# A planned order of attention pairs with groups of two, and filler matmuls in TensorE's planned gaps, in a two-layer decode kernel

## Chip, cores, metric

One core of a Trainium2 chip (trn2). The metric is device time in microseconds of one execution. Every time quoted is from runs of state "fast" unless it is said otherwise; a median of all runs is given where it helps.

## The reference, cut to what matters

```python
# x = A_x                        four tokens (B=4, one position each), D=448
x = x + A_ref(layernorm(x), K, V, wq, wo)   # attention: 16 query heads on 8 KV heads, Dh=256,
x = x + B_ref(layernorm(x), wg, wu, wd)     #   window = last 2048 cache rows
x = x + A_ref(layernorm(x), K, V, wq, wo)   # the same caches and weights again: layer 1
x = x + B_ref(layernorm(x), wg, wu, wd)     # feed-forward, F=1792, silu(x wg) * (x wu) @ wd
```

There are 4 tokens x 8 KV heads x 2 layers = 64 "pairs" of attention. A pair reads 1 MB of K and 1 MB of V. Layer 1 reads what layer 0 read, so a cache half (512 KB) that stays in SBUF saves a load.

## The kernel before

The kernel is a graph of operations with planned durations. A list scheduler written in Python orders them for each engine, gives loads one of 27 half-tiles, and places semaphore waits; the chip then runs five fixed instruction streams. The parts that matter (cuts marked `# ...`):

```python
NPOOL = 27                       # half-tiles of 512 KB
KEEP_K = 5; KEEP_V = 5           # heads per token whose K / V stay for layer 1
KLEAD = 2.2; KTAIL = 0.4; VLAG = 1.3; SLEAD = 2.5; FR = 8.4; FRD = 8.4; WOR = 0.4
ROWF = (0, 1, 2)                 # tokens whose feed-forward runs in row form

def schedule(self, npool):
    # ... at each step: the engine that is free first takes the ready operation of lowest rank
            o = min((o for o in avail[e] if ready_at[o] <= t + 1e-9), key=lambda o: (o.rank, o.i))
            if o.cell is not None:                 # a cache load: the half-tile that comes free first
                slot = min(pool)
                pool.remove(slot)
                # ... the load waits for the operation that releases this half-tile
            avail[e].remove(o)
            o.start = t
            free[e] = t + o.dur
    # ...

def pair(pos, si, side, nside, t, layer, kvh):     # one token, layer, head
    # two K loads, each followed by a VectorE transpose:
    g.op(DVE, 1.18, pos, tr, w=(kk[hf],))
    # two V loads; then on PE 32 score matmuls (8 columns of weights, 128 moving columns)
    o = g.op(PE, 0.87, pos - SLEAD, scores, r=tuple(kk) + (f"qe{q_}",), w=(f"s{s_}",), bank=(f"S{s_}",))
    if not keep_k: o.rel = tuple(kc)               # scores release K
    # max (VectorE), spread (PE), negated max (VectorE), exp (ScalarE), turn (PE), copy (ScalarE),
    # sum (PE, VectorE), then 2 x 8 value matmuls, which release V, and the combine
    # (ScalarE copy, VectorE subtract, PE flip, VectorE scale)

def steps():   # tokens two by two: layer 1 of token t-1 beside layer 0 of token t, shifted by three heads
    ...
```

Of the kernel before, what the change touches and what calls it, by code (L numbers as in the profile page):

```python
# [26 lines left out]
KEEP_K = 5  # L27
KEEP_V = 5
SHIFT = 3


KLEAD = 2.2
KTAIL = 0.4
VLAG = 1.3
SLEAD = 2.5
FR = 8.4
FRD = 8.4
WOR = 0.4
# [3 lines left out]
NY = 3  # L42
TRP = 1
LAND = 1.5
DSTART = 2.1
ROWF = (0, 1, 2)
MMV = 0.034
FAR = 1e30
TAIL = {"pe": 0.2, "dve": 0.12, "act": 0.15, "pool": 0.1, "sp": 0.05}
# [8 lines left out]

class Op:
    __slots__ = ("i", "eng", "dur", "rank", "emit", "deps", "succ", "nbytes", "dsem", "dval",  # L60
                 "start", "end", "pos", "waits", "inc", "val", "known", "run", "cell", "rel")

    def __init__(self, i, eng, dur, rank, emit):
        self.i, self.eng, self.dur, self.rank, self.emit = i, eng, dur, rank, emit
        self.deps = {}
        self.succ = []
        self.nbytes = 0
        self.dsem = None
        self.dval = 0
        self.cell = None  # L70
        self.rel = ()
        self.inc = False
        self.val = 0
        self.waits = []


class Graph:
    def __init__(self):
        self.ops = []
        self.writer = {}  # L80
        self.readers = {}
        self.banks = {}
        self.dcount = {}
# [6 lines left out]
    def op(self, eng, dur, rank, emit, r=(), w=(), bank=(), acc=()):  # L90

        o = Op(len(self.ops), eng, dur, rank, emit)
        self.ops.append(o)
# [39 lines left out]
    def schedule(self, npool):  # L133
        same = 0.08
        for o in self.ops:
            for d in o.deps:
                d.succ.append(o)
# [9 lines left out]
        order = {e: [] for e in avail}  # L147
        n = 0
        while n < len(self.ops):
# [16 lines left out]
            if o.cell is not None:  # L166
# [5 lines left out]
                if slot[2] is not None:  # L172
                    o.deps[slot[2]] = True
            avail[e].remove(o)
            o.start = t
            free[e] = t + o.dur
            o.end = t + o.dur
            if o.nbytes:
                chan = max(chan, t + DSTART) + o.nbytes / 16 * (0.007 / o.run + 1 / 26.6e3)
                o.end = chan + LAND - TAIL[SP]  # L180
# [15 lines left out]
        self.span = max(o.end for o in self.ops)  # L196
        self._place_waits()

# [46 lines left out]
def orders():  # L245



    keep = max(KEEP_K, KEEP_V)
    tail = list(range(SHIFT))  # L250
    first, second = [], []
    order = list(range(HKV))
    for t in range(B):
        first.append(order)
        mid = order[HKV - keep:] + [h for h in order[:HKV - keep] if h not in tail]
        mid = [h for h in mid if h not in tail]
        second.append(mid + tail)
        order = tail + mid
    return first, second


def steps():



    first, second = orders()
    out = [((0, 0, h),) for h in first[0]]
    for t in range(1, B):
        for i, h in enumerate(first[t]):
            if i >= SHIFT:  # L270
                assert second[t - 1][i - SHIFT] == h
                out.append(((t - 1, 1, h), (t, 0, h)))
            elif t > 1:
                assert second[t - 2][HKV - SHIFT + i] == h
                out.append(((t - 2, 1, h), (t, 0, h)))
            else:
                out.append(((t, 0, h),))
    out += [((B - 2, 1, h),) for h in second[B - 2][HKV - SHIFT:]]
    return out + [((B - 1, 1, h),) for h in second[B - 1]]


def build(nc, A_x, A_k_cache, A_v_cache, A_wq, A_wo, B_x, B_w_gate, B_w_up, B_w_down, out):
# [3 lines left out]
    with ExitStack() as es:  # L286
# [10 lines left out]
        tiny = sb("tiny", [128, 12 + NS], BF16)  # L297
        onesb, qmask, osel, rsel = tiny[:, 0:1], tiny[:, 2:6], tiny[:, 6:8], tiny[:, 8:12]
        pmax = [tiny[:, 12 + s:13 + s] for s in range(NS)]
        far = sb("far", [128, 16, 2], BF16)  # L300
        tsel = sb("tsel", [128, 4, B], BF16)
        selt = [sb(f"selt{h}", [128, 2, 4, 2, 2], BF16) for h in range(2)]
        small = sb("small", [128, 11 + 2 * NS + 4 * NY + B + 4], FP32)
        rmask = small[:, 11 + 2 * NS + 4 * NY:11 + 2 * NS + 4 * NY + B]
        rvec = small[:, 11 + 2 * NS + 4 * NY + B:11 + 2 * NS + 4 * NY + B + 4]
        nmask = small[:, 9 + 2 * NS + 4 * NY:11 + 2 * NS + 4 * NY]
        onesf, wrow, lomask = small[:, 0:1], small[:, 1:5], small[:, 5:6]
        expo = small[:, 6 + 2 * NS + 4 * NY:9 + 2 * NS + 4 * NY]
        negm = [small[:, 6 + 2 * i:8 + 2 * i] for i in range(NS)]
        rs = [small[:, 6 + 2 * (NS + i):8 + 2 * (NS + i)] for i in range(NY)]  # L310
        ri = [small[:, 6 + 2 * (NS + NY + i):8 + 2 * (NS + NY + i)] for i in range(NY)]
        qc = [sb(f"qc{t}", [128, HKV, 8, 2], BF16) for t in range(B)]
        qe = [sb(f"qe{i}", [128, 8, 4, 2], BF16) for i in range(NQ)]
        qS = sb("qS", [128, 128], BF16)
# [7 lines left out]
        xe = sb("xe", [128, 2, B], BF16)  # L322
# [5 lines left out]
        praw = [sb(f"praw{s}", [128, 258], BF16) for s in range(NS)]  # L328
        pT = [sb(f"pT{s}", [128, 2, 2, 4, 2, 2], BF16) for s in range(NY)]
        oh = [sb(f"oh{s}", [128, DH], BF16) for s in range(2)]  # L330
# [26 lines left out]
        def c_fill(e):  # L357
            e.memset(onesf[:, :], 1.0)
            e.memset(expo[:, 0:1], -0.5)
            e.memset(expo[:, 1:3], -1.0)  # L360
# [5 lines left out]
            e.memset(xn[:, :, :], 0.0)  # L366
            return e.memset(Ab[:, :], 0.0)
# [7 lines left out]
        for a in range(4):  # L375
            g.op(DVE, 0.1, R0, lambda e, a=a: e.memset(qmask[32 * a:32 * a + 32, a:a + 1], DH ** -0.5), r=("qmask",),
                 w=(f"qmask{a}",))
        ivt = identb[:, :].rearrange("p (h x z n) -> p h x z n", h=2, x=2, n=2)
        for h in range(2):
            for y in range(2):  # L380
                for x in range(2):
                    g.op(DVE, 0.1, R0, lambda e, h=h, y=y, x=x: e.tensor_copy(selt[h][:, x, :, y, :], ivt[:, h, x, 0:4, :]),
                         r=("identb",), w=(f"selt{h}{y}{x}",))
        idq = identb[:, :].rearrange("p (q z n) -> p q z n", q=4, n=2)
        g.op(DVE, 0.2, R0, lambda e: e.tensor_reduce(
            nmask[:, :], idq[:, :, 0:4, :].rearrange("p q a n -> p n q a"), AX.XY, ALU.add), r=("identb",), w=("nmask",))
        g.op(DVE, 0.1, R0, lambda e: e.tensor_reduce(negm[0][:, 0:1], nmask[:, :], AX.X, ALU.add), r=("nmask",), w=("negm0",))
        g.op(DVE, 0.1, R0, lambda e: e.tensor_scalar(negm[0][:, 1:2], negm[0][:, 0:1], -2.0, 1.0, op0=ALU.mult, op1=ALU.add),
             r=("negm0",), w=("negm0",))
        g.op(DVE, 0.1, R0, lambda e: e.tensor_scalar(  # L390
            far[:, :, :], nmask[:, :].unsqueeze(1).broadcast_to([128, 16, 2]), negm[0][:, 1:2], FAR, op0=ALU.add, op1=ALU.mult),
            r=("nmask", "negm0"), w=("far",))
        for s_ in range(NS):
            g.op(DVE, 0.2, R0, lambda e, s_=s_: e.memset(Sb[s_][:, :], 0.0), w=(f"s{s_}",), bank=(f"S{s_}",))
            g.op(DVE, 0.2, R0, lambda e, s_=s_: e.memset(praw[s_][:, :], 0.0), w=(f"praw{s_}",))
# [6 lines left out]
        iv = identb[:, :].rearrange("p (j y n) -> p j y n", j=4, n=2)  # L402
        g.op(DVE, 0.2, R0, lambda e: e.tensor_reduce(
            osel[:, :], iv[:, :, 0:2, :].rearrange("p j y n -> p n j y"), AX.XY, ALU.max, negate=True), r=("identb",),
            w=("osel",))
        g.op(DVE, 0.2, R0, lambda e: e.tensor_reduce(lomask[:, :], iv[:, :, 1, :], AX.XY, ALU.add), r=("identb",),
# [33 lines left out]
        def norm(t, rank, x):  # L440
# [15 lines left out]
            vec(rank, lambda e: e.tensor_copy(s[:, 12:14], Z2[:, 0:2]), ("z2",), (k + "m",), 0.09, ("Z2",))  # L456
# [30 lines left out]
        def qproj(ts, rank):  # L487
# [39 lines left out]
            vec(rank, lambda e: e.tensor_copy(qS[:, 0:32 * n], Zb[:, 0:32 * n]), ("z",), ("qS",), 0.12, ("Z",))  # L527
# [10 lines left out]
            g.op(PE, 0.45, rank, select, r=("qS", "identb"), w=("z2",), bank=("Z2",))  # L538
# [176 lines left out]
        first, second = orders()  # L715
        seq = [p for s in steps() for p in s]
# [6 lines left out]
        def pair(pos, si, side, nside, t, layer, kvh):  # L723
            p_, s_, q_ = pos % NY, pos % NS, pos % NQ
            if layer == 1 and (t, kvh) in k_held:
                kc, kk = k_held.pop((t, kvh))
            else:
                kc, kk = [[], []], [f"k{pos}_{hf}" for hf in range(2)]
                ksrc = A_k_cache[t, kvh, s0:s0 + WIN, :].rearrange("(p j) d -> p (j d)", p=128)
                for hf, cell in enumerate(kc):  # L730
                    g.dma(pos - KLEAD if pos <= LAST1 else pos + KTAIL, 1 << 19, lambda e, cell=cell, hf=hf: e.dma_start(  # L731
                        half[cell[0]][:, :], ksrc[:, 2048 * hf:2048 * hf + 2048]), None, w=(kk[hf],), run=4096, cell=cell)

                    def tr(e, cell=cell):
                        a = half[cell[0]][:, :].bitcast(UINT32).rearrange("p (k s) -> p k s", k=32)
                        return e.transpose(a, a)  # L736
                    g.op(DVE, 1.18, pos, tr, w=(kk[hf],))
            if layer == 1 and (t, kvh) in v_held:
                vs = v_held.pop((t, kvh))
            else:  # L740
# [240 lines left out]
```

## Time and profile before

| | before |
|---|---|
| time, median of 3 runs | 321.62 us (319.07 to 321.64); 320.86 of 4 with the run beside the changed kernel |
| profiled span | 318.6 us |
| loaded | 105.16 MB, mean 330 GB/s |
| cache loads | 88 K halves, 88 V halves |
| busy: PE / VectorE / ScalarE / GpSimd | 70 / 65 / 24 / 28% |

The lines of this profile are in the prediction. How to read them: busy shares are averages over the whole span, so the slices and windows are read for *where* the transfer engines are not full. After the last load has landed, only work that no load can hide is left; below this is called the tail.

### The profile page before, as it was taken

How to read it: one execution, taken by the hardware profiler on the slowest of the kernel's cores; microseconds unless marked ns; L12 is line 12 of the kernel's file. 1: busy time of each engine (PE TensorE's matmuls, PEld its weight loads, DVE VectorE, ACT ScalarE, POOL GpSimd, SP SyncE). 2: the span in 40 equal slices, each digit the busy share in tenths (PEclk: the TensorE clock that was granted, in tenths of full speed). 3: DMA queues.
4: the chain of work that ended last, by engine and by line, in shares of the span. 5: the costliest groups of instructions: out<-in, count | busy, mean ns of one | idle time of the engine just before them, and what ended most of it. 6: DMA issues, size and time to landing. Idle time of an engine off the chain costs nothing.

```text
span 318.6 us, 11163 instructions
## 1 busy us (share of the span) xinstructions
PE 224.0 (70%) x4840; PEld 138.0 (43%) x4840; DVE 206.8 (65%) x651; ACT 76.5 (24%) x222; POOL 89.1 (28%) x227
## 2 busy tenths in 40 slices
PE   1557546555448899687878786877689659779865
PEld 0225323223114565354346454443466337346544
DVE  7295654555244678978667878785767676565542
ACT  0023111221012233323232332231323311123420
POOL 1703121112101333242314332513143412225330
PEclk9999999999999655859595957595855855595975
DMA  7999999999998999999999999999979996668000
GB/s 272 335 406 394 393 394 396 395 394 328 318 398 331 325 391 402 397 393 388 395 338 376 362 408 398 363 358 395 345 270 335 398 387 239 244 210 306 21 3 3
DMA packets 42369, 105.16 MB, mean 330 GB/s; under 512 B 3144, under 2 KB 7248, under 8 KB 41936
## 3 DMA queue, kind: packets, MB, share of 16 engines
q1 hardware_dynamic: 42320, 104.45, 89.0%
q8 instruction: 38, 0.62, 0.8%
q14 instruction: 11, 0.09, 0.1%
HBM read 104.44 MB, written 0.00 MB: 328 GB/s over the span
## 4 chain that ended last, share of the span: by engine, by line
DMA 46%; PE 25%; SPq 15%; DVE 10%; issue 3%; ACT 1%; POOL 0%
DMA half<-in_A_k_cache_dram 22%; DMA half<-in_A_v_cache_dram 19%; PE Y L816 7%; SPq L731 6%; SPq L744 6%; DVE half L736 6%; PE S L757 6%; DMA wg_sb<-in_B_w_gate_dram 5%; SPq L415 3%; PE Z L566 3%; PE A L868 1%; PE Z L620 1%; DVE oh L830 1%; PE Z L450 1%; PE Y L793 1%
## 5 line engine op out<-in xcount | busy, mean ns | idle before, releaser
L736 DVE STREAM_TRANSPOSE half<-half 128x1024 uint32<-128x1024 uint32 x88 | 109.0, 1238 | 24.9 <-DMA half<-in_A_k_cache_dram 24.5
L816 PE MATMUL Y<-half,pT 128*4 128x256 bf16 x1024 | 60.6, 355 | 18.3 <-DMA half<-in_A_v_cache_dram 14.9
L826 POOL TENSOR_TENSOR small<-small 128x2 f32<-128x2 f32 x64 | 44.2, 694 | 78.2 <-DVE small L808 76.9
L757 PE MATMUL S<-half,qe 128*8 128x128 bf16 x2048 | 57.1, 273 | 11.8 <-DVE half L736 7.9
L757 PEld LDWEIGHTS S<-half,qe 128*8 128x8 bf16 x2048 | 43.0, 105 | 18.0 <-DVE half L736 10.2
L761 POOL TENSOR_TENSOR qe<-qc,tiny 128x64 bf16<-128x64 bf16 x64 | 18.6, 292 | 85.0 <-PE S L757 65.3
L828 ACT ACTIVATE oh<-Y 128x256 bf16<-128x256 f32 x64 | 24.5, 383 | 70.5 <-PE Y L816 70.3
L783 ACT ACTIVATE praw<-S,small 104x128 bf16<-104x128 f32 x64 | 23.0, 367 | 57.9 <-DVE small L780 56.9
L768 DVE TENSOR_REDUCE tiny<-S 104x1 bf16<-104x128 f32 x64 | 18.4, 288 | 26.2 <-PE S L757 25.7
L816 PEld LDWEIGHTS Y<-half,pT 128*4 128x4 bf16 x1024 | 21.5, 93 | 31.8 <-DMA half<-in_A_v_cache_dram 20.0
L830 DVE SCALAR_TENSOR_TENSOR oh<-oh,small,Y 128x256 bf16<-128x256 bf16 x64 | 29.7, 468 | 7.1 <-ACT oh L828 6.4
L800 ACT ACTIVATE pT<-Y 128x64 bf16<-128x64 f32 x64 | 14.0, 222 | 42.3 <-PE Y L793 37.6
L836 PE MATMUL Y<-tiny,oh 128*128 128x2 bf16 x128 | 13.1, 172 | 11.0 <-DVE oh L830 10.3
L793 PE MATMUL Y<-selt,praw 104*128 104x32 bf16 x256 | 17.3, 187 | 3.5 <-ACT praw L783 2.4
L868 PE MATMUL A<-wo_sb,oT 128*4 128x448 bf16 x140 | 16.4, 465 | 4.3 <-DVE oT L841 4.1
L793 PEld LDWEIGHTS Y<-selt,praw 104*128 104x128 bf16 x256 | 11.5, 104 | 15.2 <-issue 9.4
L772 PE MATMUL S<-far,identb 104*104 104x32 bf16 x64 | 15.0, 239 | 3.1 <-DVE tiny L768 2.1
L836 PEld LDWEIGHTS Y<-tiny,oh 128*128 128x128 bf16 x128 | 8.1, 105 | 20.9 <-DVE oh L830 14.4
L780 DVE TENSOR_REDUCE small<-S 104x1 f32<-104x32 f32 x64 | 11.6, 184 | 7.2 <-PE S L774 5.2
L803 PE MATMUL Y<-pT,tiny 128*128 128x32 bf16 x64 | 12.3, 197 | 5.0 <-ACT pT L800 4.5
L467 POOL TENSOR_SCALAR st<-st 128x1 f32<-128x1 f32 x16 | 4.2, 264 | 36.6 <-DVE st L456 36.5
L450 PE MATMUL Z<-st,small 128*128 128x2 f32 x32 | 9.1, 355 | 7.5 <-DVE st L447 6.4
(123 smaller groups left out, 256.6 us busy)
## 6 DMA issues: line engine op xcount, KB each, us to landing
half<-in_A_k_cache_dram SPq DMA_DIRECT2D x88, 512.0 KB, 8.1
half<-in_A_v_cache_dram SPq DMA_DIRECT2D x88, 512.0 KB, 7.8
wo_sb<-in_A_wo_dram SPq DMA_DIRECT2D x8, 448.0 KB, 12.6
wq_sb<-in_A_wq_dram SPq DMA_DIRECT2D x3, 1024.0 KB, 7.0
wd_sb<-in_B_w_down_dram SPq DMA_DIRECT2D x1, 1568.0 KB, 18.5
wg_sb<-in_B_w_gate_dram SPq DMA_DIRECT2D x1, 1344.0 KB, 15.5
wu_sb<-in_B_w_up_dram SPq DMA_DIRECT2D x1, 1344.0 KB, 16.0
wq_sb<-in_A_wq_dram SPq DMA_DIRECT2D x2, 256.0 KB, 10.5
```

The lines of the kernel that those rows point to most:

```text
L731: g.dma(pos - KLEAD if pos <= LAST1 else pos + KTAIL, 1 << 19, lambda e, cell=cell, hf=hf: e.dma_start(half[cell[0]][:, :], ksrc[:, 2048 * ...
L736: return e.transpose(a, a)
L744: g.dma(pos + VLAG, 1 << 19, lambda e, cell=cell, hv=hv: e.dma_start(half[cell[0]][:, :].rearrange("p (a g d) -> p a g d", a=2, g=4), vsrc ...
L757: last = e.matmul(Sb[s_][qd:qd + 8, 0:128], lhsT=qe[q_][:, ce, :, :].rearrange("p a n -> p (a n)"), rhs=kt[:, ce // 2, ce % 2, 2 * x:2 * x ...
L783: g.op(SCA, 0.38, pos, lambda e: e.activation(praw[s_][0:104, 2:258].rearrange("p (g r h l) -> p h g r l", g=2, h=2, l=2)[:, 0, :, :, :], ...
L793: last = e.matmul(Yb[p_][:, 64 + 32 * c:96 + 32 * c], lhsT=praw[s_][0:104, c0:c0 + 128], rhs=selt[h][0:104, :, :, :, :].rearrange("p x a y ...
L816: last = e.matmul(Yb[p_][32 * gg:32 * gg + 4, 256:512], lhsT=pT[p_][:, gg % 2, gg // 2, 2 * hv + a, :, :].rearrange("p y n -> p (y n)"), r ...
L826: g.op(POOL, 0.69, pos, lambda e: e.tensor_tensor(ri[p_][:, :], rs[p_][:, :], expo[:, 1:3], op=ALU.pow), r=(f"rs{p_}", "expo"), w=(f"ri{p_ ...
L828: g.op(SCA, 0.34, pos, lambda e: e.activation(oh[pos % 2][:, :], Yb[p_][:, 256:512], ACT.Copy), r=(f"y{p_}",), w=(f"oh{pos % 2}",), bank=( ...
L830: g.op(DVE, 0.43, pos, lambda e: e.scalar_tensor_tensor(out=oh[pos % 2][:, :], in0=oh[pos % 2][:, :], scalar=lomask[:, 0:1], in1=Yb[p_][:, ...
L836: last = e.matmul(Yb[p_][:, 2 * dh:2 * dh + 2], lhsT=oh[pos % 2][:, :].rearrange("p (m e) -> p e m", e=2)[:, dh, :], rhs=osel[:, :], start ...
L868: last = e.matmul(Ab[32 * k:32 * k + B, 0:D], lhsT=oT[si % 2][:, k % 2, k // 2, :], rhs=wo_sb[:, 4 * kvh + k, :], start=False, stop=False, ...
```

## The change

Intent: let the transfers run without holes, and keep PE's clock up. The core of the diff (the table of load offsets, the changed leads `KLEAD` to `WOR`, other constants and set-up code cut):

```diff
-KEEP_K = 5
-KEEP_V = 5
+KEEP_K = (5, 5, 4, 5)            # per token
+KEEP_V = (5, 5, 5, 3)
-ROWF = (0, 1, 2)
+ROWF = (0, 1)
+OFF = { ("k", 0, 0, 0): 1, ... }  # 75 offsets of single loads
+PLAN = (                          # token, layer, head; "+" joins two pairs to one group
+    "000", "002+001", "004 005", "006", "003 007", "101", "100 102", "013", ...
+    "213 215 305", "303 217+307", "214+304 300", "212", "216 211", "210", "312+314", "315 311",
+    "313+317", "316 310",
+)
+FILL0 = 12; FILLD = 0.43; FILLB = 62; HOLD = 10; HOLD_MIN = 0.8
+PAGE = 256; FETCH = (5.9, 3.6)    # a planned delay of PE's instruction stream
 ...
+            soon = [ready_at[p] for p in avail[e] if t + 1e-9 < ready_at[p] < t + o.dur - HOLD_MIN
+                    and p.rank < o.rank - HOLD]
+            if soon and e != SP:                       # "holding": wait for the more urgent operation
+                fits = [p for p in avail[e] if ready_at[p] <= t + 1e-9 and t + p.dur <= min(soon) + HOLD_MIN]
+                if not fits:
+                    free[e] = min(soon)
+                    continue
+                o = min(fits, key=lambda o: (o.rank, o.i))
 ...
+    def _fill(self):               # after scheduling: into each planned PE gap of 0.53 us or more
+        ...
+        def whole(e):              # before 62 us (planned): one matmul of 512 columns, weight zero
+            return e.matmul(Ab[:, 0:512], lhsT=zero[:, 0:1].broadcast_to([128, 128]), ..., start=False)
+        def quarters(e): ...       # later: four of 32 weight columns each
```

Groups of two share one maximum, exponential, turn, sum and combine. The fillers add zero to the bank of residual sums. To make room in SBUF, the exponent and combine buffers become single (they were two each), and there are two probability tiles instead of three.

## The prediction

> **What bounds the kernel now.** I read the page's slices first, then the busy-time windows cut at places where the slices change, then the chain of work that ended last, and at last the timeline of one late stall. The slices:
>
> ```profile
> PE   1557546555448899687878786877689659779865
> PEclk9999999999999655859595957595855855595975
> DMA  7999999999998999999999999999979996668000
> GB/s 272 335 406 394 393 394 396 395 394 328 318 398 331 325 391 402 397 393 388 395 338 376 362 408 398 363 358 395 345 270 335 398 387 239 244 210 306 21 3 3
> ```
>
> One slice is 8 us. DMA is full from slice 1 to about slice 28, has holes in slices 29 to 36, and is empty in the last three. No compute engine is near full (PE 70%, VectorE 65%). So this is a stream of cache loads with a hole near its end and a tail behind it. The windows give sizes:
>
> ```profile
> 0.00:16.00 16.00, 4.83 (x28) 2.95 (x28) 8.64 (x73) 0.78 (x1) 6.44 (x25) 1.00 0.86 304
> 16.00:72.00 56.00, 31.76 (x588) 18.11 (x588) 35.83 (x71) 10.68 (x31) 9.47 (x21) 1.00 1.04 396
> 72.00:96.00 24.00, 12.64 (x168) 5.97 (x168) 9.13 (x32) 2.59 (x6) 3.63 (x10) 1.00 1.06 349
> 96.00:112.00 16.00, 13.60 (x321) 7.86 (x317) 9.18 (x26) 4.60 (x12) 4.31 (x14) 0.81 0.91 327
> 112.00:160.00 48.00, 40.04 (x814) 22.85 (x814) 37.92 (x109) 13.96 (x43) 16.11 (x37) 0.64 1.03 395
> 160.00:224.00 64.00, 50.22 (x1182) 30.86 (x1181) 48.70 (x145) 19.79 (x58) 20.68 (x52) 0.73 1.01 375
> 224.00:296.00 72.00, 54.94 (x1331) 37.44 (x1324) 48.27 (x158) 18.39 (x56) 22.74 (x59) 0.64 0.83 299
> 296.00:318.60 22.60, 15.95 (x430) 11.99 (x428) 9.18 (x45) 5.76 (x18) 5.72 (x11) 0.75 0.01 4
> ```
>
> The last three columns are granted clock, DMA share and GB/s. A full stretch shows a share of about 1.045 (packets of neighbours overlap), so idle DMA time is length x (1 - share/1.045): 2.8 us at the start, 2.1 in 96 to 112, 0.7 in 112 to 160, 2.1 in 160 to 224, and **14.8 in 224 to 296**. The dip to 349 GB/s in 72 to 96 is no hole: the share is 1.06, the feed-forward weights come in shorter rows. Then 22.6 us of **tail** without loads. Real transfer work: 318.6 - 22.5 - 22.6 = 273.5 us for 105.16 MB.
>
> Why there is a hole: the queue waits for buffers. Of 27 half-tiles, ten K and ten V halves are kept for a token's second layer; from the last token's first-layer attention until its second layer starts, only seven circulate. The second layer waits for a chain of residual, norm, feed-forward and q projection. The timeline shows what delays that chain:
>
> ```profile
> 270.33 1.65 PE L647 MATMUL Z<-wide,wd_sb 128*128 128x2 bf16 x56
> 273.34 1.25 DVE L736 STREAM_TRANSPOSE half<-half 128x1024 uint32<-128x1024 uint32 x1 [2.60 <-DMA half<-in_A_k_cache_dram]
> 274.51 0.12 DVE L655 TENSOR_TENSOR xr<-xr,Z 128x4 f32<-128x4 f32 x1
> ```
>
> Next, two pieces of the chain of work that ended last:
>
> ```profile
> 276.82 4.50 DMA half<-in_A_k_cache_dram
> 281.33 1.25 DVE half L736
> ```
>
> Read both together: the down projection ended at 272.0; VectorE, in fixed order, sat before a transpose until its K landed at 273.3, so the residual add came 2.5 us late. The chain's two pieces show a late load and its transpose setting the pace again (first number start, second length, both in us).
>
> **The clock.** The page's clock of 9 in slices 0 to 12 must not be believed: the groups by form in two stretches say otherwise.
>
> ```profile
> L816 PE MATMUL Y<-half,pT 128*4 128x256 bf16 x64 | 4.8, 399 | 5.2 <-DMA half<-in_A_v_cache_dram 5.2
> L816 PE MATMUL Y<-half,pT 128*4 128x256 bf16 x32 | 1.6, 303 | 0.0
> ```
>
> The first is the stretch 40 to 64 us, the second 96 to 104: the same matmul takes 399 ns and then 303 (a mean over the change of state). In the timeline the q projection's 12 matmuls of 512 columns take 1.45 us at 97.6 and 0.81 at 99.1. PE was cold for 98 us, and the record of its clock starts only with the first transition.
>
> **What the Trainium skill says.** (1) "TensorE: Matmul & The Clock Gate", Part 1: the default clock is half, about 3.4 us of sustained activity releases it, and an idle window of about the same length halves it again. The trace agrees: the first release comes with the dense projection at 98 us, and afterwards the clock alternates (0.50 to 1.00 in 4 us windows). (2) "Perfetto Trace Analysis", Identifying the Most-Contended Engine: matmul busy share is a poor measure of the bound, DMA is judged by bandwidth. Hence I weigh 396 GB/s over PE's 70%. (3) "DMA: Bandwidth & Descriptors", Where 436 GB/s comes from: a fabric ceiling of 435 and an HBM limit near 358 GB/s. The trace holds 394 to 396 for 56 us, above the second figure; the measurement decides, and I use 394.
>
> **The change part by part**, counted in the instruction order of both kernels.
> - *More loads.* Kept K halves fall from 40 to 38, kept V halves from 40 to 36, so K loads go from 88 to 90 and V loads from 88 to 92: six more of 524 KB = 3.15 MB, at 394 GB/s **+8.0 us** of transfer work: 281.5 us.
> - *More room.* For the last token kept halves fall from 20 to 16, so 11 instead of 7 circulate just where the hole is. The plan also puts four pairs of token 2 between the last first-layer pair of token 3 and its second layer, instead of three: about one pair (2.1 MB, 5.3 us of transfer) more cover for the chain. The scheduler now also holds an engine idle when a more urgent operation is due soon, which is the remedy for the 2.5 us shown above. I expect the hole of 14.8 us to shrink to **6** and the smaller ones (4.9) to **3**. This is a judgement; the three causes account for about 5.3 + 2.5 + the use of four more buffers.
> - *Groups of two.* Only six of the 64 pairs' groups are doubles (58 groups for 64 pairs). Each saves one maximum, one negation, one sum and one combine on VectorE: 0.288 + 0.184 + 0.179 + 0.468 = 1.1 us, less what wider operands cost; six times, under 6.7 us on VectorE, against which two more transposes add 2 x 1.24 = 2.5. ScalarE saves at most 6 x (0.383 + 0.367 + 0.222) = 5.8 us. All beside the transfers: **0** directly, except in the tail.
> - *The tail.* Before, the last loads are K and V of the last pairs: after 296 there still come scores, softmax and values until 304.4, then output projection, norm and feed-forward. After, the last six loads are all V, the last pair has both operands kept, and doubles 312+314 and 313+317 thin the end. What remains behind the last V is values, combine and projection (303.80 to 305.9 in the old timeline, about 2.5) plus the fixed part from 305.6 to 318.6 (13): some 16 to 17.5. I take **17**, a gain of 5.6.
> - *Token 2's feed-forward* becomes the column form: PE 1.28 + 0.53 + 1.26 + 0.51 + 1.65 = 5.2 us instead of about 5.5, and two row evacuations fewer (0.54 + 0.61 + 0.35 us each): a chain shorter by some 3 us, part of the hole counted above.
> - *Fillers.* 48 matmuls of 512 columns in the first 62 us and 24 groups of four quarter-width ones, mostly in the waits of the feed-forwards. A round of 512 columns costs about 0.43 us cold (1.45 us for three rounds with the drain) and 0.21 warm, so the 48 fill 10 to 21 us of the 24 us that PE idles in 16 to 72. They should warm PE from about 20 us on. But DMA is full there, so what warmth saves (399 against about 300 ns) is hidden: **0**, within 1 us either way.
>
> Sum of the span: 281.5 + 2.8 + 3 + 6 + 17 = 310.3. The timed runs lie above the profiled span (320.69 against 318.6 in the profiled one, 321.62 the median), so I add about 1 us net of the known spread: **311 us**.
>
> **Rivals.**
> - *The holes stay.* If buffers are not the limit but the second-layer chain is, the extra 8 us only fills part of the hole and moves the rest: 281.5 + 2.8 + 4.9 + 10 + 20 = 319, within 2%. For it: in 224 to 296 PE is at 76% and cold half of the time. Against: in that window PE and VectorE both have idle time before loads.
> - *The plan is nearly perfect.* Offsets for single loads look tuned one by one; with no hole and a tail of 16 the span is 300 to 301, timed about 303. For it: 112 to 160 shows that this pipeline can hold a share of 1.03 in the busy phase.
> - *Fillers get in the way.* They are placed by planned gaps; where PE is late they cost up to 0.43 us each and make PE wait for readers of the shared bank. If one in four of the 72 lies on the path: 18 x 0.3 = 5 us, giving 316. For it: PE's order is fixed. Against: most lie before 62 us, where full queues absorb a late PE.
>
> **Range and chances.** Half the spread comes from the late hole (0 to 12 us), half from the tail (16 to 20): 304 to 318. Faster by over 2% means under 315.2; the first and third rivals lie near or above it. Slower by 2% would need the holes to stay, the tail to stay and fillers to cost as well.
>
> **What would show it.** Right: DMA packets of about 108.3 MB; a share above 0.93 from 224 us to the last load; the last load landing near 293; 16 to 18 us from there to the end; value matmuls near 300 ns instead of 399 in 40 to 64 us while GB/s there stays at 394 to 396. Wrong: a share still near 0.83 late (hole not filled), scores after the last landing (tail not shortened), or less than 390 GB/s in 16 to 72 (the fillers delay the release of buffers).

## The result, and the profile after

The changed kernel takes 311.99 us (median of 4 runs, 310.69 to 312.68). The ratio to the kernel before is **0.9726** (95% interval 0.9669 to 0.9784). Ratios here are the mean time of one kernel's fast runs over that of the other's in the same rounds, so not quite the ratio of the medians quoted. The profiled span is 309.8 us; 310.3 was the predicted sum.

The same slices of the kernel after (each now 7.7 us):

```profile
PE   0578686776779787799788798788988787986976
PEclk9999759796577897956787777655857955596975
DMA  7999999999999999999999999999899999899200
GB/s 265 333 383 399 389 403 403 393 394 351 332 394 391 392 394 399 376 381 375 373 369 380 399 397 399 393 395 351 310 382 401 396 393 401 297 324 390 85 3 3
```

The holes of slices 29 to 36 are gone but for two weak places of two slices each (351 and 310 GB/s in slices 27 and 28, 297 and 324 in 34 and 35). The granted clock changes from slice 4 on; the page of before showed no change until slice 13.

The windows of the kernel after, cut as before, but the late one cut near the last landing (288):

```profile
16.00:72.00 56.00, 42.05 (x611) 17.39 (x614) 31.24 (x65) 10.29 (x27) 9.74 (x22) 0.88 1.04 396
96.00:112.00 16.00, 13.39 (x366) 7.86 (x358) 12.70 (x33) 4.92 (x15) 5.02 (x14) 0.88 1.02 391
160.00:224.00 64.00, 52.95 (x1266) 33.44 (x1254) 45.17 (x143) 16.57 (x51) 21.18 (x54) 0.71 1.00 376
...
224.00:288.00 64.00, 52.76 (x1212) 33.69 (x1206) 46.91 (x137) 16.05 (x48) 21.49 (x57) 0.68 1.01 372
288.00:309.80 21.80, 16.36 (x416) 11.30 (x404) 8.57 (x42) 4.52 (x14) 4.99 (x10) 0.72 0.03 9
```

In 16 to 72 us DMA stays at 396 GB/s, though PE is now busy for 42.05 us there instead of 31.76: those are the fillers. The late share rises from 0.83 to 1.01. But the tail is 21.8 us by this cut, hardly shorter.

To compare kernels I count the same thing more finely in every profile: over windows of 1 us, idle is the sum of 1 - share/1.045 (share capped at 1.045), and the last landing is the end of the last window with a share above 0.3. Transfer work is what is left of the time before the last landing. The cap and the window length shift such a sum by perhaps 2 us, and the work column scatters by that much, so only larger differences are used. ("Late" is 224 us to the last landing.)

| profiled run | span | work | idle to 224 | idle late | tail |
|---|---|---|---|---|---|
| before | 318.6 | 271.3 | 9.6 | 14.2 | 23.6 |
| after | 309.8 | 276.9 | 8.8 | 3.4 | 20.8 |
| difference | -8.8 | +5.6 | -0.8 | -10.8 | -2.8 |

Where the tail went, from the timeline of the kernel after:

```profile
283.74 1.25 DVE L822 STREAM_TRANSPOSE half<-half 128x1024 uint32<-128x1024 uint32 x1
...
287.38 0.68 PE L852 MATMUL S<-half,qe 128*8 128x128 bf16 x32
...
290.99 0.64 PE L852 MATMUL S<-half,qe 128*8 128x128 bf16 x32
...
295.80 0.61 PE L942 MATMUL Y<-half,pT 128*4 128x256 bf16 x16
...
300.04 1.20 PEld L702 LDWEIGHTS Z<-xn,wg_sb 128*128 128x128 bf16 x42 [0.42 <-DVE st L538]
```

The last transpose starts at 283.7, the last load lands near 289 (by the fine count above), and scores (L852) still run at 291: the values of five pairs are still to come (8 matmuls for each half of V) and end at 296.4. (At 300.0 the weight loads of the last feed-forward begin.) That is the sign that the prediction named for "tail not shortened".

The groups by form in 40 to 64 us of the kernel after show the clock (columns: busy us, mean ns of one, idle before):

```profile
L1068 PE MATMUL A<-identb,small 128*128 128x512 bf16 x19 | 7.6, 476 | 0.0
L942 PE MATMUL Y<-half,pT 128*4 128x256 bf16 x32 | 1.6, 303 | 0.7 <-DMA half<-in_A_v_cache_dram 0.7
```

A value matmul takes 303 ns where it took 399: the fillers (L1068) do raise the clock.

And the delay that the prediction showed before is still to be found at the last norm chain, once, in the timeline of the kernel after:

```profile
278.29 0.54 PE L987 MATMUL A<-oT,wo_sb 128*128 128x1 bf16 x16
...
280.63 1.25 DVE L822 STREAM_TRANSPOSE half<-half 128x1024 uint32<-128x1024 uint32 x1 [2.00 <-DMA half<-in_A_k_cache_dram]
281.79 0.12 DVE L760 TENSOR_TENSOR xr<-xr,A 128x4 f32<-128x4 f32 x1
```

The projection ended at 278.8, the residual add came at 281.8, behind a transpose that sat waiting for its load. Holding works on planned times; here the load came later than planned: in the plan that the kernel computes when it is built, this transpose begins 0.19 us before the projection ends, on the chip 1.8 us after.

### The profile page after: what moved, and what is told of

It reads as the page before. It is cut to its first block, busy times and chain, and to the rows that moved or that the text cites. A ratio compares the mean times of both kernels' runs of the same rounds, so it can differ in the third digit from the quotient of the medians.

```text
span 309.8 us, 11390 instructions
## 1 busy us (share of the span) xinstructions
PE 240.2 (78%) x4972; PEld 136.9 (44%) x4972; DVE 202.1 (65%) x641; ACT 70.0 (23%) x203; POOL 88.3 (28%) x233
## 2 busy tenths in 40 slices
DMA packets 43746, 108.33 MB, mean 350 GB/s; under 512 B 3240, under 2 KB 7344, under 8 KB 43312
## 4 chain that ended last, share of the span: by engine, by line
DMA 35%; PE 32%; SPq 15%; DVE 11%; issue 5%; ACT 1%; DVEq 0%
DMA half<-in_A_k_cache_dram 20%; DMA half<-in_A_v_cache_dram 13%; PE Y L942 8%; DVE half L822 6%; SPq L830 5%; SPq L817 5%; PE S L852 5%; SPq L497 4%; PE Z L586 4%; PE Z L702 2%; DVE oh L959 2%; DMA wg_sb<-in_B_w_gate_dram 2%; PE Z L729 2%; PE A L995 1%; PE Z L532 1%
## 5 line engine op out<-in xcount | busy, mean ns | idle before, releaser
L822 DVE STREAM_TRANSPOSE half<-half 128x1024 uint32<-128x1024 uint32 x90 | 110.5, 1234 | 23.6 <-DMA half<-in_A_k_cache_dram 23.3
L955 POOL TENSOR_TENSOR small<-small 128x2 f32<-128x2 f32 (+1 forms) x58 | 42.5, 735 | 81.1 <-DVE small L933 79.4
L942 PE MATMUL Y<-half,pT 128*4 128x256 bf16 (+1 forms) x1024 | 55.1, 324 | 12.2 <-DMA half<-in_A_v_cache_dram 6.9
L852 PE MATMUL S<-half,qe 128*8 128x128 bf16 x1664 | 41.6, 251 | 5.0 <-DVE half L822 2.3
L852 PEld LDWEIGHTS S<-half,qe 128*8 128x8 bf16 x1664 | 29.6, 95 | 10.1 <-DVE half L822 3.8
L942 PEld LDWEIGHTS Y<-half,pT 128*4 128x4 bf16 (+1 forms) x1024 | 20.1, 89 | 24.6 <-DMA half<-in_A_v_cache_dram 12.1
L876 DVE TENSOR_REDUCE tiny<-S 104x1 bf16<-104x128 f32 (+1 forms) x58 | 16.9, 294 | 9.2 <-PE S L852 9.0
L920 ACT ACTIVATE pT<-Y 128x64 bf16<-128x64 f32 (+1 forms) x58 | 13.6, 234 | 27.8 <-PE Y L912 27.5
L1068 PE MATMUL A<-identb,small 128*128 128x512 bf16 x48 | 19.8, 528 | 0.0
L912 PE MATMUL Y<-sel,praw 104*128 104x32 bf16 x208 | 14.1, 184 | 3.3 <-ACT praw L898 2.8
L586 PE MATMUL Z<-wq_sb,xn 128*4 128x512 bf16 x120 | 14.1, 601 | 0.3 <-DVE st L538 0.3
```

Source lines behind the costliest of these rows:

```text
L586: last = e.matmul(zb[32 * j:32 * j + B, 0:512], lhsT=lhsT, rhs=wq_sb[:, c:c + 512], start=(cc == 0), stop=(cc == 3), skip_group_check=True)
L822: return e.transpose(a, a)
L852: last = e.matmul(Sb[s_][qd:qd + 8, 0:128], lhsT=qe[q_][:, 0, ce, :, :].rearrange("p a n -> p (a n)"), rhs=kt[:, ce // 2, ce % 2, 2 * x:2 ...
L942: last = e.matmul(Yb[p_][32 * gg:32 * gg + M, 256:512], lhsT=pT[pt][:, gg, 2 * hv + a, 4 * P:4 * P + M] if n == 2 else p1[:, gg % 2, gg // ...
L955: g.op(POOL, 0.69, pos, lambda e: e.tensor_tensor(ri[p_][:, 0:2 * n], rs[p_][:, 0:2 * n], expo[:, 1:1 + 2 * n], op=ALU.pow), r=(f"rs{p_}", ...
L1068: return e.matmul(Ab[:, 0:512], lhsT=zero[:, 0:1].broadcast_to([128, 128]), rhs=identb[:, :].unsqueeze(1).broadcast_to([128, 4, 128]), sta ...
```

## The experiments

Theory P is the prediction's: loads, room and plan bring the gain, fillers nothing. The rivals: F (the warm clock brings it), G (groups of two), O (no part by itself, but an order that was tuned as a whole).

### 1. No fillers

```diff
-FILL0 = 12
+FILL0 = 1e9
```

> The changed kernel without any of its 72 fillers; all other instructions keep their order. Theory P (prediction: loads, buffers and plan bring the gain, fillers nothing because DMA is full while they run): ratio to the kernel before stays 0.97 to 0.98, GB/s in 16 to 72 us stays 394 to 396, while value matmuls in 40 to 64 us go back to about 400 ns. Rival F (warmth brings the gain): ratio returns to 0.99 or more, DMA share before 112 us falls. Rival C (fillers cost): under 0.967.

Measured: 313.08 us, ratio **0.9756** (0.9707 to 0.9805). Without fillers a value matmul in 40 to 64 us takes 412 ns:

```profile
L942 PE MATMUL Y<-half,pT 128*4 128x256 bf16 x24 | 1.7, 412 | 0.1
```

GB/s in 16 to 72 us is 395. All three are as P forecast. Rival F falls: with a cold PE the gain stays. The fillers' worth, 0.3%, is within the interval. The other engines carry the same operations in the same order, and every load goes into the same half-tile (only waits differ), so this is the cleanest ablation.

### 2. The old plan with fillers, and without

Both kernels are the changed code with the old plan, leads, keeps and row form, no holding, no offsets and no planned delay of PE's stream (`FETCH`); their load order is that of the kernel before, entry for entry. The second also has `FILL0 = 1e9`.

> The old plan, old leads, old keeps and old feed-forward form in the new code, no holding, no single offsets, with fillers (35 whole, 55 groups of four). Load order is that of the kernel before, entry for entry. Theory P: ratio 0.99 to 1.01. Rival F: 0.96 to 0.98.

> The run with the old plan in the new code, this time without fillers. It tells apart what made that run 3% slower than before (328.3 us, late hole 20 us): if fillers on a plan they don't fit cost (rival C), this one comes back to 0.99 to 1.01; if it is the new code (one exponent buffer, one combine buffer, two instead of three probability tiles), it stays at 1.02 to 1.04. Theory P gives no number here.

Measured: with fillers ratio **1.0301** (1.0201 to 1.0401); without **1.0502** (1.0421 to 1.0584). The profiled run of the second fell in the slow state. Two things follow. First, theory P failed on the number for the old plan: I had expected 0.99 to 1.01 with fillers. The new code with the old plan is some 5% slower than the old code with it. Second, in this plan the fillers are worth about 2%, and the two intervals do not overlap (the runs were on different chips, each beside the kernel before). "Fillers give nothing" holds for the tuned plan; it is not a property of fillers. Why they help here is not shown. It can't be the full queue of the first stretch alone: in 16 to 72 us both old-plan kernels move 396 GB/s. They part later (377 against 362 GB/s in 112 to 160), and after 62 us this plan has 55 groups of fillers where the tuned one has 24; but the second profile is the slow one, so it can't settle this. What exactly costs 5% is open, too: one exponent and one combine buffer instead of two, and a few changed planned durations, came together.

### 3. Keeps: room against bytes

Ten K and ten V halves kept for every token, in the changed kernel; and the other way round, the kernel before with the changed keeps:

```diff
-KEEP_K = (5, 5, 4, 5)
-KEEP_V = (5, 5, 5, 3)
+KEEP_K = (5, 5, 5, 5)
+KEEP_V = (5, 5, 5, 5)
```

```diff
+KKT, KVT = (5, 5, 4, 5), (5, 5, 5, 3)
-            ... for k in (KEEP_K, KEEP_V))
+            ... for k in (KKT[t], KVT[t]))
```

> The changed kernel with ten K and ten V halves kept for every token: 88 + 88 loads as in the kernel before instead of 90 + 92, 3.15 MB less, seven circulating halves for the last token instead of eleven. If room is worth more than bytes (P): hole late grows, ratio 0.98 to 1.00. If the extra bytes were simply a price (rival B): 8 us less transfer work, ratio 0.95 to 0.96.

> The kernel before with the changed kernel's numbers of kept halves per token and nothing else (90 + 92 loads). If room alone fills the hole (P's strongest cause): ratio 0.98 to 0.99 in spite of 8 us more transfer work. If room helps only with the plan and order of loads fitted to it: 1.00 to 1.02.

Measured: **0.9838** (0.9758 to 0.9918) for the first; **1.0056** (0.9994 to 1.0118) for the second. In the first, transfer work falls by 7.4 us and the late idle time rises from 3.4 to 9.8, the tail from 20.8 to 23.4; its late window:

```profile
224.00:289.00 65.00, 54.90 (x1194) 33.81 (x1195) 43.95 (x136) 15.20 (x45) 21.78 (x57) 0.66 0.89 327
```

So fewer bytes were not faster: what was saved in transfer came back as waiting, as P said. (The new keeps also reorder the plan; experiment 7 shows what that alone can cost.) But in the old plan the same room fills nothing (late idle 12.7 us against 14.2), and 3.15 MB more are simply carried. In these two plans, room helped only with the order fitted to it.

### 4. Groups of two: split them, or make more

```diff
-    "002+001", ... "204+115" ... "217+307", "214+304 300" ... "312+314" ... "313+317"
+    "002 001", ... "204 115" ... "217 307", "214 304 300" ... "312 314" ... "313 317"
```

```diff
-... "312+314", "315 311", "313+317", "316 310",
+... "312+314", "315+311", "313+317", "316+310",
```

> The changed kernel with the six groups of two split into singles, same order of pairs. P: their work lies beside the transfers, ratio 0.97 to 0.98, tail at most 1 us longer. Rival G (groups matter in the busy end): ratio 0.985 or more, tail 3 us or more longer.

> The changed kernel with the last token's remaining single pairs grouped too (four doubles at the end instead of two). If splitting the doubles cost 4 us of tail because their small operations are on the path there, two more doubles shorten the tail of 20.8 us by 1 to 3 us: ratio 0.963 to 0.97. If a double has to wait for its later load, the tail gets longer: 0.975 or more.

Measured: all single **0.986** (0.9799 to 0.992); four doubles at the end **0.9703** (0.961 to 0.9795), 310.77 us. The windows from the last landing to the end, all single first, then the changed kernel, then four doubles:

```profile
290.00:314.90 24.90, 18.89 (x491) 12.93 (x487) 9.97 (x47) 6.05 (x19) 6.05 (x12) 0.77 0.03 8
```

```profile
289.00:309.80 20.80, 15.36 (x393) 10.88 (x385) 7.86 (x38) 4.11 (x13) 4.77 (x9) 0.71 0.02 4
```

```profile
288.00:307.50 19.50, 13.93 (x365) 10.01 (x357) 6.13 (x32) 3.02 (x8) 4.50 (x8) 0.76 0.02 6
```

With 0, 2 and 4 doubles at the end the tail is 24.9, 20.8 and 19.5 us; VectorE has 9.97, 7.86 and 6.13 us of work in it, PE 18.89, 15.36 and 13.93. P missed: it gave the single pairs 0.97 to 0.98 and at most 1 us more tail, and the tail is 4.1 us longer. This is the monotone picture that rival G asks for; it points to doubles on the path in the tail. Two things weaken it. Regrouping also reorders the engines, which experiment 7 shows can cost as much by itself. And the other profiled kernels of the changed code that keep the two doubles have tails of 20.4 to 23.4 us, so 24.9 stands out by 1.5 us only, and 19.5 by 0.9. What speaks for the groups is that work and tail fall together. The last step does not show in the time: 0.9703 and 0.9726 cannot be told apart.

### 5. Holding

Taken out of the changed kernel (`HOLD = 1e9`), and added alone to the kernel before (the seven lines of the diff above that hold an engine, and their two constants).

> The changed kernel whose scheduler never holds an engine for a more urgent operation. P counted 2.5 us for it in the late hole: ratio about 0.98. If holding does nothing: 0.97 to 0.976. If the order was tuned around it: 0.985 or more.

> The kernel before with the holding rule of the changed scheduler added, nothing else (old plan, keeps and leads). If holding cures late residual adds by itself: ratio 0.975 to 0.99 and a smaller late hole. If it works only in the plan that was tuned with it: 1.00 to 1.03.

Measured: without it **0.9982** (0.9914 to 1.005), the whole gain gone; alone in the kernel before **0.9915** (0.9843 to 0.9988), late idle 10.7 us instead of 14.2. The late window of the second:

```profile
224.00:291.00 67.00, 56.10 (x1337) 37.30 (x1333) 46.43 (x152) 19.51 (x58) 22.13 (x58) 0.63 0.88 321
```

Holding alone is worth about 1%, not the 2.6 points that its removal costs. P had given about 0.98 for the removal and missed; the 0.9915 lies just above the range for a cure by itself (0.975 to 0.99).

### 6. Offsets of single loads

```diff
-OFF = { 75 entries }
+OFF = {}
```

> The changed kernel without the offsets of single loads (74 entries), so loads go out by the general leads alone; bytes and keeps are the same. Theory P did not count them. If the plan and the keeps carry the gain: 0.97 to 0.98. If the tuned order of loads carries it (rival O): 0.99 to 1.01, with idle DMA time back by 5 us or more.

Measured: **1.011** (1.0055 to 1.0164), by its interval slower than before, and even past the range that I had given rival O. (The table has 75 entries, not the 74 of my text.) In 16 to 112 us idle goes from 1.2 to 6.2 us, late idle from 3.4 to 10.5:

```profile
16.00:112.00 96.00, 69.68 (x1137) 30.94 (x1141) 52.20 (x119) 15.54 (x42) 17.35 (x44) 0.76 0.99 364
```

Theory P, which had not counted the offsets, is refuted on this point.

### 7. One planning number

If taking out holding costs the whole gain and taking out the offsets costs more than the whole, the parts do not add. So: does a part's removal cost what the part gives, or only the tuned order? Two kernels with *all* parts and one planned duration altered:

```diff
-                        g.op(DVE, 1.18, pp, tr, w=(kk[hf],))
+                        g.op(DVE, 1.24, pp, tr, w=(kk[hf],))
```

```diff
-MMV = 0.034
+MMV = 0.036
```

> The changed kernel with one planning number altered: the planned length of a transpose 1.24 us (as measured) instead of 1.18. Same loads in the same order, same parts, but 760 lines of PE's order and 658 of VectorE's differ. It measures how much of a removed part's cost is only the loss of a tuned order. If the parts themselves carry the gain: within 0.5% of the changed kernel (0.968 to 0.978). If a tuned order carries it (rival O): 0.985 or more.

> The changed kernel with another planning number altered a little: a weight-bound matmul counted as 36 instead of 34 ns. Same loads, some 88 lines of difference on PE and on VectorE. Parts carry the gain: 0.968 to 0.978; tuned order: up to 0.985.

Measured: transposes planned at 1.24 us, which is what they take: **0.9973** (0.9891 to 1.0055), 319.62 us. The second number: **0.9735** (0.9641 to 0.9829). The first alteration loses the whole gain with no part taken away. Loads still go out in the same order, but when buffer numbers are compared, about half of them go into another half-tile, so they wait for another release; the second alteration left those assignments as they were. It also changed far less of the engines' order (some 88 lines on PE against 760), so the assignment and the order are not told apart. One stall of the first kernel, from its timeline, the queue's waits (us in total, times, longest; 112 to 160 us) and its windows:

```profile
123.70 7.52 SPq L830 DMA_DIRECT2D half<-in_A_v_cache_dram  x2
```

```profile
SPq L830 <- PE S L852: 7.2, 2, 6.7
```

```profile
128.00:132.00 4.00, 3.90 (x83) 2.31 (x80) 3.55 (x10) 1.03 (x4) 1.93 (x4) 0.50 0.32 117
```

Two V loads occupied the queue for 7.52 us from 123.7 on, most of it waiting for scores to release a half-tile; nothing behind them could be issued, and DMA fell to 117 GB/s. Idle to 224 us is 11.7 here (8.8 in the changed kernel), late 9.1 (3.4).

The other kernels can be sorted in the same way. Built again from their code, those that keep the changed kernel's order of cache loads put this many of the 182 loads into another half-tile: no fillers and the second number 0, four doubles 1; no holding 72, all single 89, transposes at 1.24 us 102. The first three have ratios of 0.9703 to 0.9756, the last three 0.986 to 0.9982. That fits a cost of the assignment, but the order on the engines changed along with it; no run changed one without the other.

## Why the prediction was right, point by point

- **The total** (311 predicted, 311.99 measured; span 310.3 against 309.8): right, but by terms that partly cancel. That it came within 1 us is luck.
- **More loads, 3.15 MB:** right in bytes (105.16 to 108.33 MB). As time, 8.0 us predicted, 5.6 by the fine count, within its error.
- **The late hole** (14.8 to 6 us): it shrank further, 14.2 to 3.4 by the fine count. The share in 224 us to the last load is 1.01, above the 0.93 named.
- **The other holes** (7.7 to 5.8 us, the start among them): hardly changed, 9.6 to 8.8 by the fine count.
- **The tail** (22.6 to 17): this is the term that was mis-sized; 23.6 to 20.8. The step "what remains behind the last V is values, combine and projection" failed. Scores of backlogged pairs still ran at 291.0, 2.0 us after the last landing. The last *loads* were V, as the instruction order said, but PE was five pairs of values behind them. This backlog is planned: in the kernel's own plan the last load lands at 278.2 us and the last scores start at 279.5. The fixed part was about right: from the end of the last values to the end of the span it took 14.2 us before (304.4 to 318.6) and 13.4 after (296.4 to 309.8). From the last landing to the end of the last values it took 7.4 us (9.4 before), where 17 - 14.2 leaves 2.8. As far as experiment 4 shows, the gain there is came with the doubles, which the prediction named but did not separate.
- **The last landing** (293 predicted): it came at 289. This balances the tail, by luck.
- **Fillers, 0 within 1 us:** right here (0.3%, unresolved), and the reason given fits: PE warm or cold, DMA is full in 16 to 72 us. In the old plan the same statement would be wrong (2%), though DMA is just as full there in 16 to 72 us; so a full queue in that stretch is not enough to say it.
- **The causes of the filled hole** ("5.3 + 2.5 + four more buffers"): not shown as a sum. Room alone does nothing to the old plan, holding alone gives 0.9%, and the offsets stood only in the rival of a near-perfect plan. One altered planning number loses 2.5 points (0.9973 less 0.9726) with all parts present. So what the removals lose, counted the same way (holding 2.6, offsets 3.8, groups 1.3, keeps 1.1 points), is the part's worth mixed with the loss of a tuned order. What is shown is that the late hole closes when all of them are fitted together; how much each would give after a new tuning without it stays open. The new leads, the row form, the planned delay of PE's stream and the order of pairs in `PLAN` were never varied alone.
- **Slips that did not decide it:** 303.80 to 305.9 is 2.1 us, not "about 2.5", so the tail's own sum begins at 15, not 16. PE was cold for more than "half of the time" late: a mean of 0.64 between readings of 0.50 and 1.00 is some 72% at 0.50. That shorter rows cause the dip in 72 to 96 us was not tested.
- **Rivals:** "fillers get in the way" is not seen in this plan. "The holes stay" (319) would have been right for several neighbours of this plan: without offsets, without holding and with the 1.24 us, late idle is 7.3 to 10.5 us and the span 319.5 to 320.9.

A version clearly better than the changed kernel was not found. Four doubles at the end gave 310.77 us; to call it faster needs more runs than these.

## What to carry to other kernels

In a kernel that lives from a statically planned stream of loads, count transfer work, holes and tail separately: here, 3.15 MB fewer to move did not pay, because the late hole came back with them (experiment 3). Before you credit a part of a tuned schedule with what its removal costs, alter one planning number that should not matter: if that costs as much, the removal may have measured the tuning. And look for the tail in the backlog at the last landing, not in which load comes last.

## What the Trainium skill lacked or had wrong

- "TensorE: Matmul & The Clock Gate", Part 1, warns that clock records can be unreliable, but not that the clock reads full until the first recorded change. Here it read 1.00 up to 96 us in the kernel before, while value matmuls took 399 to 406 ns there and 303 ns around the first change. Without the fillers they took 420 ns in 40 to 60 us at a mean reading of 0.91.
- The same page and part ties the clock to how busy PE has been. Here PE was busy 15.01 of 16 us in 112 to 128 us of the kernel before at a granted clock of 0.55 (busy spans are modelled, so idle slots inside them are not excluded). How much activity is enough is given no number.
- The same page does not say whether a zero weight counts as activity. It does here: a run of 15 fillers with zero weight over 5.86 us from 23.06 us on brought their mean from 626 ns (24 to 28 us) to 421 (28 to 30) and then about 380 ns. Without fillers PE was busy for 0.85 of the 8 us from 22 to 30. Only the weights are zero; the moving operand is the identity matrix.
- "DMA: Bandwidth & Descriptors", Where 436 GB/s comes from, lets an HBM limit near 358 GB/s bind for such loads. Both kernels held 396 GB/s for 56 us. The sentence there is too strict for a core that runs alone, as here; the page's own table of measurements just above it, for a single core, does go higher.
- No page says that a plan of fixed instruction streams can lose 2.5 points (0.9726 to 0.9973) from one planned duration changed by 0.06 us.
